# Attention pieces of later batches moved to other steps of two dense layers, and a few clears and loads issued later

## The chip, the cores and the metric

The kernel runs on one core of a Trainium2 chip, in one launch. The metric is the device time of one execution in microseconds (us). The kernel before has a median of 334.19 us over 3 runs (332.76 to 334.4). The engines' names in the profile are PE (TensorE, matmuls; PEld is its weight load), DVE (VectorE), ACT (ScalarE), POOL (GpSimd) and SP (SyncE). POOL and SP here mostly start DMAs. Each engine has one list of instructions, which it works off in the order in which the program issued them.

## The reference

```python
# q, k, v: (8 batches, 8 heads, 576 positions, 64), float32
scores = q @ k^T / 8                       # per batch and head
rel = i - j
heads 0..3:  keep 0 <= rel < 32
heads 4..7:  keep 0 <= rel < 128 and rel % 4 == 0
attn = softmax(scores where kept, else -1e9)
x = (attn @ v) as (4608 tokens, 512)
h = x @ w_in                               # 512 -> 2048
out = (h / (1 + exp(-h))) @ w_out          # 2048 -> 512, float32
```

## The kernel before

**Attention.** A batch `b` is worked in two halves `z`: `z = 0` are the plain heads 0 to 3, `z = 1` the dilated heads 4 to 7, whose positions are sorted into four classes by position modulo 4. For a half, these steps follow each other:

- `load_qk(b)` and `load_v(b)`: DMAs issued by POOL, 8 for q and k, 5 for v. `shift_v(b, ...)` copies parts of v to other partitions by DMA.
- `transpose(b, z, which, copies)`: PE turns q (`which = 0`) or k (`which = 1`) so that the head dimension lies on partitions (line 274, 36 or 24 small matmuls). The result, in two PSUM tiles, is copied to SBUF by `copies[0]` and `copies[1]` (line 278 for z = 0, line 287 for z = 1). `both` means one copy on DVE and the other on ACT.
- `scores(b, z)`: 72 or 80 small matmuls on PE (lines 324 and 336), then on DVE mask and scale (L448, L457) and a row maximum (L464).
- `exps(b, z, hi)`, once for `hi = 0` and once for `hi = 1`: 8 or 10 exponentials on ACT, each of 128x64 with its row sum (L496: one ACTIVATE and one ACTIVATION_READ_ACCUMULATOR). Where `shift` has subtracted the maximum on DVE beforehand (L474), it is one exponential of 128x640 (L487), and the sum is made on DVE (L505).
- `later(...)` holds the rest: `normal` (DVE: 1/sum and multiply, L509 to L512), `turn` (PE transposes, L521), `turned` (the copy of these, L529), `values` (PE, L554 and L618), `finish` (copies to `xT`, L631, L623, L625).

PSUM for all of this is a pool `ps` of 4 buffers. Where a tile takes a buffer again, the writer waits until every reader of the tile before is done; the same holds for the two buffers `n0`, `n1` of q and k.

**Dense layers.** For every batch, layer one makes 16 tiles `h` (L644, in batch 0 in two parts by `layer1_part`, L664), each followed by a SiLU on ACT into `gT` (L652, L671). Layer two multiplies `gT` with `w_out` into 128x512 tiles `o` (L705; in batch 0 L681), which DVE copies out (L690) and SP stores. PSUM for `h` and `o` is a pool `big` of 2 buffers.

**Order.** Batch 0's attention stands in a written-out list ahead of the loop. Everything else is spread by hand: `plan_of(b)` registers calls with `at(step, function, ...)`, and the loops over the dense layers of batch `b` call `plan(step)` ahead of each piece of their own work. Calls of one step are issued in the order in which they were registered. For batches 1 to 7 steps 0 to 15 stand ahead of the 16 tiles of layer one, and step 16 + n ahead of the n-th group of four matmuls of layer two. In batch 0 layer one runs from step -16 to 15, two steps to one call of `layer1_part` (two tiles of half a batch), and layer two again from 16. Steps that the loops don't reach are issued at the end of the batch. What a call issues goes to the end of each engine's list: a copy on ACT in step 17 stands behind every exponential of step 16.

The pieces that the change touches: `transposes(at, b, z, step)` issues both transposes of a half with `both` as copies, `all_exps(b, z)` puts the exponentials of a half at step 16, and `later(at, b, z, steps)` puts `normal` of `hi = 0` and `1` at the first two steps, `turn` and `turned` at the third, `values` and `finish` at the fourth. `clear_v(1, nc.vector)` is four memsets on DVE (L194 to L197) in the v buffer of batch 1.

Of the kernel before, what the change touches and what calls it, by code (L numbers as in the profile page):

```python
# [28 lines left out]
def kernel(  # L29
# [9 lines left out]
    nc = tc.nc  # L39
# [55 lines left out]
    def load_qk(b):  # L95

        for which in (0, 1):
            t = nat.tile([P, H * 8, D], F16, tag=f"n{which}", name=f"n{which}_{b}")
            u0, u1 = 2 * URS[0], 2 * (URS[0] + URS[1])
            qk[b, 0, which] = t[:, 0:u0].rearrange("p (h u) d -> p h u d", h=2)  # L100
            qk[b, 1, which] = t[:, u0:u1].rearrange("p (h u) d -> p h u d", h=2)
        for z in (1, 0) if b == 1 else (0, 1):
            for which, src in ((1, k), (0, q)):
                for i in (0, 1):
                    h = 2 * (2 * z + i)
                    nc.gpsimd.dma_start(  # L106
                        out=qk[b, z, which][i * HF : i * HF + UPS[z]].rearrange("p h u d -> p h (u d)"),
                        in_=src[b, h : h + 2].rearrange("h (p u) d -> p h (u d)", u=URS[z]),
                    )
# [13 lines left out]
    def load_v(b, pieces=("first", "second", "short", "plain")):  # L123
        vw = vws[b % 2]
        for m in (0, 1):
            if ("first", "second")[m] in pieces:
                nc.gpsimd.dma_start(  # L127
                    out=vw[KB:P, NP + m * ND : NP + (m + 1) * ND].rearrange("p (h r) d -> p h (r d)", r=DIL),
                    in_=v[b, HH:H, m * DIL * KB : (m + 1) * DIL * KB].rearrange("h (p r) d -> p h (r d)", r=DIL),
                )  # L130
        if "short" in pieces:
            lo = CL - W - TL
            for n in (0, 1):
                c = NP + 2 * ND + 2 * n * DIL
                nc.gpsimd.dma_start(
                    out=vw[n * KB : n * KB + W + TL, c : c + 2 * DIL].rearrange("p (h r) d -> p h (r d)", r=DIL),
                    in_=v[b, HH + 2 * n : HH + 2 * n + 2, lo * DIL : S].rearrange("h (p r) d -> p h (r d)", r=DIL),
                )
        if "plain" in pieces:
            nc.gpsimd.dma_start(  # L140
                out=vw[KB:P, 0:NP].rearrange("r (h m) d -> r h m d", h=HH),
                in_=v[b, 0:HH].rearrange("h (m r) d -> r h m d", r=KB),
            )
# [41 lines left out]
    def load_w_out(c):  # L185
        nc.gpsimd.dma_start(  # L186
            out=w_out16[:, 4 * c : 4 * c + 4, :],
            in_=moe_w_out[c * FC : (c + 1) * FC, :].rearrange("(c p) m -> p c m", p=P),
        )


    def clear_v(b, engine):
        vw = vws[b]
        engine.memset(vw[0:W, 0:NP].rearrange("p (h m) d -> p h m d", h=HH)[:, :, 0], 0.0)  # L194
        engine.memset(vw[0:W, NP : NP + ND], 0.0)
        for n in (0, 1):
            engine.memset(vw[n * KB + W : n * KB + KB, NP + 2 * ND :], 0.0)  # L197
# [210 lines left out]
    def scaled0(z, part):  # L408
        a = att(0)
        w = width(0, z, part)  # L410
        n = stat.tile([P, WM], F32, tag="nm", name=f"nms_0_{z}_{part}")
        nc.vector.tensor_scalar(n[:, 0:w], a["nm", z, part][:, 0:w], scale, None, ALU.mult)
        a["nm", z, part] = n
# [309 lines left out]
    def transposes(at, b, z, step):  # L723
        for which in (1, 0):
            at(step, transpose, b, z, which, both)

    def later(at, b, z, steps, copies=(nc.vector.tensor_copy, nc.vector.tensor_copy)):

        for hi in (0, 1):
            at(steps[hi], normal, b, z, hi)  # L730
        for hi in (0, 1):
            at(steps[2], turn, b, z, hi)
        for hi in (0, 1):
            at(steps[2], turned, b, z, hi, copies[hi])
        at(steps[3], values, b, z)
        at(steps[3], finish, b, z, copies)

    def plan_of(b):
        ev = {}

        def at(s, fn, *args):
            ev.setdefault(s, []).append((fn, args))

        def all_exps(b, z):
            for hi in (0, 1):
                at(16, exps, b, z, hi)

        if b == 0:

            at(-16, normal, 0, 1, 1)  # L750
            at(-15, shift_class, 0, dve, 1, 2)
            at(-14, normal, 0, 0, 1)
            at(-8, turn, 0, 1, 1)
            at(-8, turned, 0, 1, 1, act)
            at(-6, values0, 1, 1)
            at(-6, last_values, 0, 1, (1,))
            at(-6, finish0, 1, 1)
            at(-6, last_finish, 0, 1, 1)
            at(-4, turn, 0, 0, 1)
            at(-4, turned, 0, 0, 1)  # L760
            at(-2, values0, 0, 1)
            at(-2, last_values, 0, 0, (1,))
            at(-2, finish0, 0, 1, both)
            at(-2, last_finish, 0, 0, 1)
            transposes(at, 1, 1, 4)
            at(7, scores, 1, 1)
            for hi in (0, 1):
                at(7, shift, 1, 1, hi)
            transposes(at, 1, 0, 9)
            at(13, scores, 1, 0)  # L770
            at(14, shift_v, 1, nc.sync.dma_start)
            at(15, load_qk, 3)
            at(15, load_v, 2)
            at(15, shift_v, 2, nc.gpsimd.dma_start)
            all_exps(1, 1)
            all_exps(1, 0)
            later(at, 1, 1, (18, 19, 23, 25), both)
            later(at, 1, 0, (20, 23, 27, 29), both)
        elif b == 1:
            at(16, load_v, 3)  # L780
            at(16, shift_v, 3, nc.gpsimd.dma_start)
            transposes(at, 2, 0, 4)
            transposes(at, 2, 1, 10)
            transposes(at, 3, 0, 15)
            at(7, scores, 2, 0)
            at(17, load_qk, 4)
            at(13, scores, 2, 1)
            all_exps(2, 0)
            all_exps(2, 1)
            at(17, scores, 3, 0)  # L790
            at(18, exps, 3, 0, 0)
            at(18, exps, 3, 0, 1)
            later(at, 2, 0, (22, 24, 27, 28))
            later(at, 2, 1, (29, 31, 33, 34))
        else:
            if b + 2 < B:
                at(16, load_v, b + 2)
                at(16, shift_v, b + 2, nc.gpsimd.dma_start)
            if b + 1 < B:
                if b == 2:  # L800
                    for n in (0, 1):
                        at(1 + 2 * n, transpose, 3, 1, 1 - n, both)
                later(at, b + 1, 0, (0, 0, 4, 6))
                if b + 3 < B:
                    at(16, load_qk, b + 3)
            if b + 2 < B:
                transposes(at, b + 2, 0, 13)
                at(17, scores, b + 2, 0)
                at(18, exps, b + 2, 0, 0)
                at(18, exps, b + 2, 0, 1)  # L810
            if b + 1 < B:
                at(9, scores, b + 1, 1)
                all_exps(b + 1, 1)
                later(at, b + 1, 1, (22, 24, 27, 28))
            if b + 2 < B:
                transposes(at, b + 2, 1, 30)

        def plan(s):
            for fn, args in ev.pop(s, ()):
                fn(*args)  # L820

        return plan


    def keep_busy(tile, n):

        for _ in range(n):
            nc.tensor.matmul(
                tile[:, 0].rearrange("p (a c) -> p a c", c=P), ident,
                ident[:, None, :].broadcast_to([P, 4, P]), start=True, stop=True,  # L830
            )
# [13 lines left out]
    exps(0, 1, 0)  # L845
    maxima0(0, 0)
    scaled0(0, 0)
    clear_v(1, nc.vector)
    load_w_out(0)
    load_w_out(1)  # L850
    load_v(1)
    load_w_out(2)
    load_w_out(3)
    for which in (1, 0):
        transpose0(1, 1, which, act)
    normal(0, 1, 0)
# [24 lines left out]
    shift0(0, 1)  # L881
    exps(0, 0, 1)
    keep_busy(warm, 2)
    load_qk(2)

    for b in range(B):
        plan = plan_of(b)
        if b == 0:
            for x in range(NFF):
                plan(2 * x - NFF)  # L890
                plan(2 * x + 1 - NFF)
                layer1_part(2 * x % NFF, 2 * x // NFF, None if x else warm)
        else:
            for f in range(NFF):
                plan(f)
                layer1(b, f)
        if b == 0:
            layer2_first(plan)
        else:
            layer2(b, plan)  # L900
        for s in range(NFF, 3 * NFF):
            plan(s)
# [30 lines left out]
```

## Time and profile before

| what | before |
|---|---|
| median of 3 runs | 334.19 us (332.76 to 334.4) |
| profiled execution, its own time | 334.39 us |
| its span, first to last instruction | 332.6 us |
| PE busy | 313.6 us, 94% |
| ACT busy | 216.3 us, 65% |
| DVE busy | 179.0 us, 54% |
| POOL busy | 83.5 us, 25% |
| mean granted TensorE clock | 0.995 |

The profile is one execution. Times in its timeline count from the first instruction. "Chain" is the work that ended last, followed back from the end; "issue" is time in which an engine waited for nothing that the profile shows. A matmul group's busy time includes a modelled end. The profiled execution's own time is 1.8 us above its span.

### The profile page before, as it was taken

What the parts mean: (1) busy time and instruction counts of PE and PEld (TensorE: products, weight loads), DVE (VectorE), ACT (ScalarE), POOL (GpSimd) and SP (SyncE); (2) the same over time, 40 slices, a digit from 0 to 9 for tenths busy, and PEclk for the clock granted to TensorE, in tenths of its full rate; (3) what the DMA queues carried; (4) which work ended last, traced back from release to release, by engine and by line L of the source; (5) the groups of instructions that cost most, each with busy time, mean ns of one, the idle gap of its engine ahead of it and who ended that gap; (6) DMA issues with size and microseconds to landing.
All of it is one profiled execution on the core that took longest, in us unless ns stands there. A gap on an engine that the chain in (4) does not pass through costs nothing.

```text
span 332.6 us, 11772 instructions
## 1 busy us (share of the span) xinstructions
PE 313.6 (94%) x5151; PEld 202.5 (61%) x5151; DVE 179.0 (54%) x375; ACT 216.3 (65%) x703; POOL 83.5 (25%) x140
## 2 busy tenths in 40 slices
PE   5779889998999999999999979999999999999995
PEld 2548554576645776467745757468745676467643
DVE  5895756535668754673476443774557442530011
ACT  2765639465799858985799337995699357826300
POOL 8447527534200560056004700041000000000000
PEclk9999979999999999999999999999999999999999
DMA  8999999993811974197317960175001100110021
GB/s 110 187 212 203 191 229 205 136 217 61 129 66 65 128 124 67 66 160 121 68 42 112 180 111 2 65 97 109 4 34 65 63 4 0 66 65 0 2 95 64
DMA packets 45524, 32.63 MB, mean 98 GB/s; under 512 B 21248, under 2 KB 40192, under 8 KB 45472
## 3 DMA queue, kind: packets, MB, share of 16 engines
q0 software_dynamic: 39520, 21.73, 47.7%
q1 hardware_dynamic: 5952, 10.14, 8.4%
q8 instruction: 40, 0.66, 0.8%
q14 instruction: 12, 0.10, 0.1%
HBM read 37.75 MB, written 9.44 MB: 142 GB/s over the span
## 4 chain that ended last, share of the span: by engine, by line
PE 79%; DMA 8%; ACT 5%; issue 3%; POOL 2%; DVE 2%; POOLq 0%
PE h L644 34%; PE o L705 31%; DMA n<-in_k_dram 4%; ACT pe L496 4%; PE t L274 3%; PE x L554 3%; DMA vw<-in_v_dram 2%; DMA n<-in_q_dram 2%; PE pt L521 2%; PE o L681 2%; PE s L336 1%; PE s L324 1%; PE h L664 1%; POOL n L118 1%; POOL w_out L186 0%
## 5 line engine op out<-in xcount | busy, mean ns | idle before, releaser
L705 PE MATMUL o<-w_out,gT 128*128 128x512 f16 (+1 forms) x528 | 115.8, 373 | 0.5 <-DVE ob_last L714 0.5
L652 ACT ACTIVATE gT<-h 128x576 f16<-128x576 f32 x112 | 73.0, 651 | 66.2 <-PE h L644 65.5
L644 PE MATMUL h<-xT,w_in 128*128 128x288 f16 x896 | 115.4, 286 | 0.0
L644 PEld LDWEIGHTS <-w_in 128*128 128x128 f16 x896 | 85.7, 98 | 23.0 <-DVE ob L690 0.3
L705 PEld LDWEIGHTS <-gT 128*128 128x128 f16 x528 | 50.1, 98 | 53.6 <-issue 0.7
L496 ACT ACTIVATE pe<-ms,nm 128x64 f32<-128x64 f32 x246 | 81.6, 334 | 0.1
L690 DVE COPY ob<-o 128x512 f32<-128x512 f32 x35 | 24.1, 690 | 52.9 <-PE o L705 50.7
L496 ACT ACTIVATION_READ_ACCUMULATOR pe<-ms,nm 128x1 f32 x246 | 46.2, 188 | 0.0
L448 DVE SCALAR_TENSOR_TENSOR ms<-s,mask 128x512 f32<-128x512 f32 x28 | 19.2, 687 | 38.5 <-PE ss L324 18.9
L127 POOL DMA_DIRECT2D vw<-in_v_dram x16 | 10.1, 638 | 89.9 <-PE x L554 88.4
L512 DVE TENSOR_TENSOR pn<-pe,r 128x640 f16<-128x640 f32 (+2 forms) x32 | 25.3, 792 | 1.1
L631 DVE CAST xT<-x 128x512 f16<-128x512 f32 x26 | 16.8, 686 | 11.2 <-PE xs L618 11.2
L464 DVE TENSOR_REDUCE nm<-ms 128x10 f32<-128x640 f32 (+1 forms) x28 | 22.0, 787 | 1.0
L664 PE MATMUL h<-xT,w_in 128*128 128x256 f16 (+1 forms) x128 | 19.6, 307 | 2.9 <-issue 2.2
L106 POOL DMA_DIRECT2D n<-in_k_dram x28 | 16.5, 602 | 10.2 <-DMA w_in<-in_moe_w_in_dram 3.7
L106 POOL DMA_DIRECT2D n<-in_q_dram x28 | 16.5, 606 | 10.4 <-DMA w_out<-in_moe_w_out_dram 5.5
L671 ACT ACTIVATE gT<-h 128x512 f16<-128x512 f32 (+1 forms) x16 | 10.3, 650 | 11.7 <-PE h L664 11.6
L664 PEld LDWEIGHTS <-w_in 128*128 128x128 f16 x128 | 12.7, 104 | 7.8 <-issue 3.9
L529 DVE COPY ptT<-pt 128x640 f16<-128x640 f16 (+1 forms) x27 | 11.8, 470 | 10.2 <-PE pt L521 10.0
L681 PE MATMUL o<-w_out,gT 128*128 128x512 f16 x64 | 14.8, 379 | 0.0
L521 PE MATMUL pt<-ident,pn 128*128 128x128 f16 x152 | 12.2, 224 | 2.7 <-DVE pn L512 2.7
L274 PEld LDWEIGHTS <-n 64*64 64x64 f16 (+1 forms) x840 | 10.1, 101 | 5.6 <-issue 3.8
(102 smaller groups left out, 269.8 us busy)
## 6 DMA issues: line engine op xcount, KB each, us to landing
out_dram<-ob SPq DMA_DIRECT2D x35, 256.0 KB, 2.0
n<-in_k_dram POOLq DMA_DIRECT2D x28, 144.0 KB, 5.5
n<-in_q_dram POOLq DMA_DIRECT2D x28, 144.0 KB, 5.9
vw<-in_v_dram POOLq DMA_DIRECT2D x8, 288.0 KB, 6.7
vw<-in_v_dram POOLq DMA_DIRECT2D x16, 128.0 KB, 4.1
w_in<-in_moe_w_in_dram POOLq DMA_DIRECT2D x4, 512.0 KB, 11.7
w_out<-in_moe_w_out_dram POOLq DMA_DIRECT2D x4, 512.0 KB, 10.2
vw<-vw POOLq DMA_DIRECT2D x12, 128.0 KB, 3.1
```

The costliest lines, as they stand in the source:

```text
L106: nc.gpsimd.dma_start(out=qk[b, z, which][i * HF : i * HF + UPS[z]].rearrange("p h u d -> p h (u d)"), in_=src[b, h : h + 2].rearrange("h ...
L274: nc.tensor.transpose(dst, w, ident[r, r])
L448: nc.vector.scalar_tensor_tensor(out=ms[:, 0:8].rearrange("p (n t) c -> p n (t c)", n=2), in0=s[hi].rearrange("p n t c -> p n (t c)"), sca ...
L464: nc.vector.tensor_reduce(out=nm[:, 0:w], in_=ms[:, 0:w], axis=AX.X, op=ALU.max, negate=True)
L496: nc.scalar.activation(pe[:, t, :], slot(t), AF.Exp, scale=1.0 if b else scale, bias=nm[:, t : t + 1], accum_out=l[:, t : t + 1],)
L512: nc.vector.tensor_tensor(pn[:, 0:w], a["pe", z, hi][:, 0:w], r[:, 0:w, None].broadcast_to([P, w, KB]), ALU.mult)
L644: nc.tensor.matmul(h[:, half, 0:HS], w_in16[:, c, f * P : f * P + P], xT[:, c, half * HS : half * HS + HS], start=(c == 0), stop=(c == MC ...
L652: nc.scalar.activation(gT[:, f, s0 : s0 + S].rearrange("p (a c) -> p a c", a=2), h[:, :, 0:HS], AF.Silu)
L664: nc.tensor.matmul(h[:, i, 0 : c1 - c0], w_in16[:, c, (f + i) * P : (f + i + 1) * P], xT[:, c, c0:c1], start=(c == 0), stop=(c == MC - 1),)
L681: nc.tensor.matmul(o, gT[:, f, t * P : (t + 1) * P], w_out16[:, f, :], start=(f == 0), stop=(f == NFF - 1),)
L690: nc.vector.tensor_copy(ob, o)
L705: nc.tensor.matmul(o[:, part, 0:m] if last else o[:, 0], gT[:, f, t * P : (t + 1) * P], w_out16[:, f, part * m : (part + 1) * m] if last e ...
```

## The change

Nothing is added to or taken from the work; calls move.

- In batch 0: `transposes(1, 1)` from step 4 to 2, `scores(1, 1)` with its two `shift` from 7 to 8, `transposes(1, 0)` from 9 to 17, `scores(1, 0)` from 13 to 21, `exps(1, 0)` from 16 to 21, and the steps of both `later` by up to 3.
- In batch 1: `transposes(2, 0)` from 4 to 2, `transposes(2, 1)` from 10 to 9, `scores(2, 0)` from 7 to 6, `transposes(3, 0)` from 15 to 17, `scores(3, 0)` from 17 to 21, `exps(3, 0)` from 18 to 21.
- In batches 2 to 6: `scores(b + 1, 1)` from step 9 to 10.
- `clear_v(1)` goes from the list ahead of the loop to step -13 of batch 0, behind `normal(0, 0, 1)`, and the calls for the loads of `w_out`, of v of batch 1 and of q and k of batch 2 move with it. The order of the DMAs on POOL's queue stays the same.

```diff
             at(-14, normal, 0, 0, 1)
+            at(-13, clear_v, 1, nc.vector)
+            at(-13, load_v, 1)
+            for c in (2, 3):
+                at(-13, load_w_out, c)
+            at(-13, load_qk, 2)
...
-            transposes(at, 1, 1, 4)
-            at(7, scores, 1, 1)
+            transposes(at, 1, 1, 2)
+            at(8, scores, 1, 1)
             for hi in (0, 1):
-                at(7, shift, 1, 1, hi)
-            transposes(at, 1, 0, 9)
-            at(13, scores, 1, 0)
+                at(8, shift, 1, 1, hi)
+            transposes(at, 1, 0, 17)
+            at(21, scores, 1, 0)
...
             all_exps(1, 1)
-            all_exps(1, 0)
-            later(at, 1, 1, (18, 19, 23, 25), both)
-            later(at, 1, 0, (20, 23, 27, 29), both)
+            for hi in (0, 1):
+                at(21, exps, 1, 0, hi)
+            later(at, 1, 1, (18, 20, 24, 26), both)
+            later(at, 1, 0, (23, 25, 28, 30), both)
         elif b == 1:
...
-            transposes(at, 2, 0, 4)
-            transposes(at, 2, 1, 10)
-            transposes(at, 3, 0, 15)
-            at(7, scores, 2, 0)
+            transposes(at, 2, 0, 2)
+            transposes(at, 2, 1, 9)
+            transposes(at, 3, 0, 17)
+            at(6, scores, 2, 0)
             at(17, load_qk, 4)
             at(13, scores, 2, 1)
             all_exps(2, 0)
             all_exps(2, 1)
-            at(17, scores, 3, 0)
-            at(18, exps, 3, 0, 0)
-            at(18, exps, 3, 0, 1)
+            at(21, scores, 3, 0)
+            at(21, exps, 3, 0, 0)
+            at(21, exps, 3, 0, 1)
...
             if b + 1 < B:
-                at(9, scores, b + 1, 1)
+                at(10, scores, b + 1, 1)
...
     scaled0(0, 0)
-    clear_v(1, nc.vector)
-    load_w_out(0)
-    load_w_out(1)
-    load_v(1)
-    load_w_out(2)
-    load_w_out(3)
...
     keep_busy(warm, 2)
-    load_qk(2)
+    load_w_out(0)
+    load_w_out(1)
```

## The prediction

> **What bounds the kernel now.** I read the page first (busy time, clock, chain), then the chain in order of time with PE's waits, then ACT's timeline where layer two of batch 1 begins, then busy time by stage. The page says that PE is the bound:
>
> ```profile
> PE 313.6 (94%) x5151; PEld 202.5 (61%) x5151; DVE 179.0 (54%) x375; ACT 216.3 (65%) x703; POOL 83.5 (25%) x140
> PE 79%; DMA 8%; ACT 5%; issue 3%; POOL 2%; DVE 2%; POOLq 0%
> q8 instruction: 40, 0.66, 0.8%
> ```
>
> PE carries 79% of the chain, so a microsecond in which PE waits is a microsecond of the time unless a later wait swallows it. In the chain in order of time (start, length, what), PE pauses in batch 0 and hardly at all from there on:
>
> ```profile
> 39.79 0.47 PE t L274 x35
> 40.26 0.51 PE h L664 x3
> 40.77 2.25 issue
> 43.02 3.24 PE h L664 x13
> ...
> 88.00 1.09 PE h L644 x8
> 89.08 0.86 PE o L705 x4
> 89.95 0.61 PE s L324 x64
> 90.56 0.08 PE ss L324 x6
> 90.64 8.74 PE o L705 x40
> ```
>
> Layer one of batch 1 ends at 89.08; one group of layer two (0.86) and the scores of batch 3's plain heads (0.69) follow without a wait. What ACT does in that place, from its timeline:
>
> ```profile
> 87.27 0.63 ACT L278 COPY kT<-t 128x576 f16<-128x576 f16 x1
> 88.13 0.64 ACT L278 COPY qT<-t 128x576 f16<-128x576 f16 x1 [0.23 <-PE t L274]
> 89.12 0.65 ACT L652 ACTIVATE gT<-h 128x576 f16<-128x576 f32 x1 [0.35 <-PE h L644]
> 89.79 1.28 ACT L496 ACT_TABLE_LOAD   x1
> 91.08 0.35 ACT L496 ACTIVATE pe<-ms,nm 128x64 f32<-128x64 f32 x1
> ```
>
> The two copies of batch 3's k and q are made before the last SiLU; from 91.08 on ACT has exponentials alone, one every 0.33 us. The table by stage says how full ACT is there (columns: PE, PEld, DVE, ACT, POOL busy, clock, DMA share, GB/s):
>
> ```profile
> 43.49:46.90 3.41, 3.41 (x83) 1.95 (x81) 0.00 (x0) 1.31 (x2) 0.56 (x1) 0.50 1.22 244
> 89.08:109.89 20.81, 20.81 (x326) 10.71 (x324) 14.85 (x34) 20.72 (x115) 1.92 (x4) 1.00 0.19 60
> ```
>
> Layer two of batch 1: PE 20.81 of 20.81 us, ACT 20.72. Neither has slack. The first row shows the clock at half speed behind the pause of 2.25 us.
>
> **Batch 1: the copies behind the exponentials (+10.4).** `transposes(3, 0)` goes from step 15 to 17. Its copies on ACT now stand behind all of step 16, which is `exps` of batch 2: 8 + 10 + 10 + 10 = 38 exponentials. `scores(3, 0)`, now at step 21, reads for its second pair of heads the kT and qT that ACT copies, and PE works in order: behind that wait stand 15 groups of layer two and the turns and values of batch 2. Counted from the end of layer one (89.08 here):
> - ACT: 2.00 to the first exponential (91.08), 38 x 0.330 = 12.54 (spacing from 91.08 to 104.35, 40 exponentials later, is 0.332), copies about 1.2. Ready at 15.8.
> - PE: five groups of step 16 to 20, 5 x 0.86 = 4.30; transposes 0.76 (72 matmuls); first half of the scores 0.32. There at 5.4.
> - Wait: 15.8 - 5.4 = 10.4 us. DVE makes its own copies at once and can't shorten it.
>
> What is late next: the mask and maximum of these scores are 3.2 us on DVE (0.69 + 0.69 + 0.68 + 0.28 + 0.82) and stand ahead of `normal(2, 0, 1)` at step 24, whose turn is at 27. PE takes about 6 us to get there; I give it 0.9 of further wait, between 0 and 2. Nothing pays the 10.4 back, since from 109.89 on PE has no wait for ACT or DVE over 0.3 us until batch 7.
>
> **The clock behind a wait (+1.0 here).** After 2.25 us of pause, the half-speed stretch from 43.49 to 46.90 took 3.24 us for 13 matmuls that take 13 x 0.136 = 1.77 at full speed: 1.5 lost. A wait of 10.4 us will bring this on too; how much of it falls on work depends on when PE resumes. Bounds 0 and two such stretches (3.0); I take 1.0, as transposes and scores hardly slow (64 score matmuls took 0.72 instead of 0.61). [...]
>
> **Batch 0: pauses out, another in (-1.3).**
> - `clear_v(1)`: four memsets, 11.72 to 13.70 on DVE, leave the path to `normal(0, 1, 0)`. The first layer-one matmul (21.57) also waits for ACT, whose exponentials end at 15.5; of 2.0 us I take 0.9 (0 to 1.5). In their new place they lie in DVE's 1.56 us of idle before 28.63; at most 0.4 us sticks out, ahead of copies into xT. POOL's loads wait for them from about 30.4 on; they are done by then.
> - Loads: the order on POOL's queue is the same and the queue is DMA-bound up to 50 us, so `load_qk(2)` and `load_w_out` cost nothing. `load_qk(3)` must now wait for the later `transposes(1, 0)`; these run at about 44, its turn on the queue comes at 48.6. Cover gone: it and `load_v(2)` would slip by the excess, and batch 3's transposes need them only 40 us later.
> - Waits inside batch 0 (21.57 to 67.68) that go: 0.80 at `transposes(1, 0)` (until 39.59, when DVE's L457 is done with a PSUM buffer of the scores before), the pause 2.25, the clock 1.5, 0.65 and 0.62 in layer two: -5.8. Six tiles of layer one now run between `transposes(1, 1)` and their scores, eight between these and `transposes(1, 0)`.
> - New: `scores(1, 0)` at step 21. From the start of layer two: five groups and transposes 5.1, scores 0.7; DVE is busy with two `normal` of batch 1 until 7.6 (from 3.1 on, 2 x 2.25); mask and maximum 1.5 with their gaps; so exponentials start at 9.1, 18 x 0.33 = 6.0; then ACT's copy of the turned half (1, 1, 1), 0.67, which stands behind them: 15.8. PE reaches `values(1, 1)` at step 26 after ten groups 8.7 + 0.76 + 0.7 + 0.56 of turns = 10.8. Wait 5.0, and half clock behind it, +0.4 (the values are small).
> - Sum -0.9 - 5.8 + 5.0 + 0.4 = -1.3, bounds -4 and +2.
>
> **The pauses called issue (-1.5).** PE pauses at 40.77 (2.25), 75.90 (0.86) and 196.24 (1.88) with nothing to wait for. The trace's packets of the instruction queue q8 (40 of 16 KB; PE has 10,302 instructions) show why: one lands at 41.64, 75.43 and 196.69, and PE goes on 1.38, 1.33 and 1.43 later; the three places lie multiples of 256 instructions apart. So PE runs dry where it uses up 256 small instructions faster than the next block lands. The change puts more large matmuls among the small ones there (scores one tile later in every batch): I take 0.7 of the 0.86 and 0.8 of the 1.88 as gained, bounds 0 and 2.7. [...]
>
> **Sum.** 10.4 + 0.9 + 1.0 - 1.3 - 1.5 = +9.5. Made against the profiled execution: 334.39 + 9.5 = 343.9 us, 0.2 above what the median of 334.19 would give.
>
> **Rivals.**
> - *Slow clock after both waits.* If each of the two waits brings two full stretches of half speed over large matmuls, 2 x 3.0 - 1.4 = +4.6: 348.5. For it: 1.5 lost after only 2.25 of pause. Against: no other pause (1.88 at 196.24 included) shows a lower clock. Chance 0.12.
> - *Smaller wait.* Batch 0 gains its full 4 and both late pauses vanish (2.7), no slow clock: 10.4 + 0.9 - 4 - 2.7 = +4.6: 339.0. Chance 0.14.
> - *Faster: ACT's copies are not late.* The place is step 17 of batch 1, the price the 12.3 us of 10.4 + 0.9 + 1.0. If ACT reached the copies by the time PE has its first half of scores, the change would be -1.3 - 1.5 = -2.8: 331.6. That needs at most 5.4 - 2.00 - 1.2 = 2.2 us of exponentials ahead of them, 6 of 38. For it: in batch 0 the same move has only two short exponentials (L487, 1.36 us) ahead of the copies, and doesn't wait. Against: the order of the calls leaves 38 in front. Chance 0.04.
> - *No change to be seen.* The wait would have to be cut to about 3 us by the same way. Chance 0.02.
>
> **How the numbers follow.** Forecast 343.9 with 0.68. A measurement of this kernel can't tell less than about 0.5% (1.7 us) from no change. The range runs from the small wait to the slow clock, 339.0 to 348.5; it leaves out the fast cases and the ends of those two. Faster 0.04, same 0.02, slower 0.94.
>
> **What would show it.** In the profile after: a wait of some 10 us of PE at L324 for ACT's copy qT L278 near 95 us; ACT's exponentials without a gap before that copy; half clock behind it; a wait of about 5 us at L554 for ptT L529 near 52 us; no pause at 40 us. Wrong if PE passes `scores(3, 0)` without that wait, or if the stages from batch 2 on are shorter by more than 2 us.

## The result and the profile after

| | before | the change | ratio (95% interval) |
|---|---|---|---|
| first comparison, median of 4 runs each | 333.69 us (332.76 to 334.4) | 344.11 us (342.33 to 347.86) | 1.0296 (1.0242 to 1.0350) |
| second comparison | 334.79 us (11 runs) | 342.27 us (6 runs) | 1.0227 (1.0190 to 1.0263) |

The change is slower by 2.3 to 3.0%; 343.9 us were forecast, with a range of 339.0 to 348.5. The execution profiled in the first comparison was the slow one of its four (347.86 us, which the ratio leaves out), so what follows reads the profile of the second comparison: 343.62 us, span 341.8, clock 0.975. It is 1.35 us above the median beside it, so differences from the profile before come out larger here (+9.2) than the second ratio gives (+7.6). From its page, busy time and the chain by engine:

```profile
PE 315.3 (92%) x5151; PEld 203.3 (59%) x5151; DVE 178.8 (52%) x375; ACT 216.2 (63%) x703; POOL 83.4 (24%) x140
...
PE 79%; ACT 12%; DVE 4%; DMA 2%; issue 2%; POOL 1%; POOLq 0%; ACTq 0%
```

The work is the same. PE is busy for 315.3 us instead of 313.6, because more of it runs at half clock: in layer two of batch 1 alone, as the row below shows, PE is busy 23.89, where the same work at full speed takes 20.80 + 0.76. In the chain, ACT has gone from 5% to 12%. PE's waits name the place (us in total, times, longest):

```profile
PE s L324 <- ACT qT L278: 9.9, 1, 9.9
...
PE x L554 <- ACT ptT L529: 2.1, 1, 2.1
PE x L554 <- DVE ptT L529: 2.0, 1, 2.0
...
PE s L336 <- issue: 0.8, 1, 0.8
```

Left out are smaller waits, those of the first 19 us, and one of 1.1 for ACT's SiLU early in batch 0 (0.7 before). The wait for the copy `qT` is new, and so is the one for DVE's copy at L554, in batch 0; the one for ACT's at L554 was 0.6 before. The pause of 2.25 us at 40.77 is gone, and the one of 1.88 at 196.24 is 0.8. The chain in order of time (start, length, what) shows the long wait from the side that causes it:

```profile
86.78 1.28 ACT L496
88.06 0.01 issue
88.07 0.81 ACT pe L496 x5
88.89 0.10 issue
88.99 3.21 ACT pe L496 x20
92.20 0.10 issue
92.30 3.21 ACT pe L496 x20
95.52 0.10 issue
95.62 5.16 ACT pe L496 x31
100.77 0.52 ACT kT L278
101.29 0.54 ACT qT L278
101.83 0.04 issue
101.88 0.41 PE s L324 x30
102.30 0.17 PE ss L324 x7
102.46 7.18 PE o L705 x24
```

5 + 20 + 20 + 31 = 76 records are 38 exponentials of two instructions each. They run from 88.07 to 100.77 with holes of 0.10 us; the two copies stand behind them, and PE's second half of scores behind the copies. The 24 matmuls of layer two behind the wait take 7.18 us; at full speed, 0.86 for four as in the chain of before, they would take 5.2.

By stages, counted from the first dense matmul of each (so the times differ a little from those of the chain):

| stage | before | the change | difference | forecast |
|---|---|---|---|---|
| up to layer one of batch 1 | 67.52 | 66.31 | -1.21 | -1.3 |
| layer one of batch 1 | 21.40 | 19.60 | -1.80 | -0.7 - 0.76 (transposes that leave) = -1.46 |
| layer two of batch 1 | 20.80 | 34.08 | +13.28 | 10.4 + 0.9 + 1.0 + 0.76 (transposes that come) = +13.06 |
| batches 2 to 7 | 222.88 | 221.81 | -1.07 | -0.8 |
| span | 332.6 | 341.8 | +9.2 | +9.5 |

The stage table's row (us; then PE, PEld, DVE, ACT, POOL busy; clock; DMA share; GB/s) for layer two of batch 1 says the same: PE was full before (20.81 of 20.81), now it is busy 23.89 of 34.08, at a mean clock of 0.85.

```profile
85.91:119.99 34.08, 23.89 (x398) 11.81 (x395) 16.61 (x36) 23.04 (x117) 1.75 (x3) 0.85 0.13 40
```

### The profile page after: what moved, and what is told of

It is laid out like the page before. It is cut to its first block, busy times and chain, and to the rows that moved or that the text cites. A ratio compares the mean times of both kernels' runs of the same rounds, so it can differ in the third digit from the quotient of the medians.

```text
span 346.1 us, 11765 instructions
## 1 busy us (share of the span) xinstructions
PE 318.4 (92%) x5151; PEld 204.5 (59%) x5151; DVE 178.9 (52%) x375; ACT 216.4 (63%) x703; POOL 83.6 (24%) x140
## 4 chain that ended last, share of the span: by engine, by line
PE 80%; ACT 11%; DVE 3%; issue 2%; DMA 2%; POOL 1%; POOLq 0%; ACTq 0%
PE h L644 33%; PE o L705 29%; ACT pe L496 8%; PE h L664 4%; PE t L274 3%; PE x L554 3%; PE pt L521 2%; PE o L681 2%; DMA n<-in_q_dram 2%; PE s L336 1%; PE s L324 1%; ACT L496 1%; DVE pn L512 1%; PE x L580 1%; POOL n L118 1%
## 5 line engine op out<-in xcount | busy, mean ns | idle before, releaser
L705 PE MATMUL o<-w_out,gT 128*128 128x512 f16 (+1 forms) x528 | 118.2, 378 | 0.5 <-DVE ob_last L714 0.5
L644 PE MATMUL h<-xT,w_in 128*128 128x288 f16 x896 | 116.9, 289 | 0.0
L127 POOL DMA_DIRECT2D vw<-in_v_dram x16 | 10.1, 636 | 102.3 <-PE x L554 100.8
L664 PE MATMUL h<-xT,w_in 128*128 128x256 f16 (+1 forms) x128 | 18.0, 297 | 0.4 <-ACT gT L671 0.4
L529 DVE COPY ptT<-pt 128x640 f16<-128x640 f16 (+1 forms) x27 | 11.8, 469 | 12.2 <-PE pt L521 12.0
L324 PE MATMUL s<-kT,qT 64*32 64x64 f16 x520 | 5.9, 203 | 12.7 <-ACT qT L278 10.4
L681 PE MATMUL o<-w_out,gT 128*128 128x512 f16 x64 | 17.0, 414 | 0.0
L324 PEld LDWEIGHTS <-qT 64*32 64x32 f16 x576 | 5.0, 93 | 16.6 <-ACT qT L278 10.5
```

The lines of the kernel that those rows point to most:

```text
L644: nc.tensor.matmul(h[:, half, 0:HS], w_in16[:, c, f * P : f * P + P], xT[:, c, half * HS : half * HS + HS], start=(c == 0), stop=(c == MC ...
L664: nc.tensor.matmul(h[:, i, 0 : c1 - c0], w_in16[:, c, (f + i) * P : (f + i + 1) * P], xT[:, c, c0:c1], start=(c == 0), stop=(c == MC - 1),)
L681: nc.tensor.matmul(o, gT[:, f, t * P : (t + 1) * P], w_out16[:, f, :], start=(f == 0), stop=(f == NFF - 1),)
L705: nc.tensor.matmul(o[:, part, 0:m] if last else o[:, 0], gT[:, f, t * P : (t + 1) * P], w_out16[:, f, part * m : (part + 1) * m] if last e ...
```

## The experiments

**Theory:** the change's other moves gain about 3 us, and one call, `transposes(3, 0)` behind 38 exponentials on ACT, costs 12 to 13. **Rivals:** PE's later scores and DVE cost it, and not the copies; or the clock behind the waits is the larger part; or the other moved steps lose as well. The kernels were timed in three groups, each on a chip of its own and beside the kernel before: experiments 1 to 4 (its median there 335.26), 6 to 9 (334.63) and 5 (334.79). Ratios are to the kernel before of the same group, and differences in us are worked out from them. What is read from a profile rests on one execution of each kernel.

**1. Back to step 15.** The change, with the one call back in its old step.

```diff
-            transposes(at, 3, 0, 17)
+            transposes(at, 3, 0, 15)
```

> The changed kernel with one edit taken back: transposes(3, 0) of batch 1 stands at step 15 again, ahead of the exponentials of step 16; scores(3, 0) and exps(3, 0) stay at 21. Theory 'queue' (ACT's two copies stood behind 38 exponentials and PE waited for them): the wait of 10.4 us at L324 and the half-speed stretch behind it (2.3 us in the profile after) are gone, 331 to 333 us. Rival 'late scores' (scores and exponentials of batch 3 at 21 are what costs, since mask, exponentials and PSUM buffers come too late for layer two): 340 us or more, with PE waiting somewhere else in layer two of batch 1.

Measured: 332.18 us, ratio 0.9909 (0.9878 to 0.9940). Its chain at the same place has no ACT in it:

```profile
87.41 4.32 PE o L705 x20
91.73 0.61 PE s L324 x64
92.34 0.08 PE ss L324 x6
92.42 0.69 DVE ms L448
```

The scores follow the five groups of layer two at once. Layer two of batch 1 takes 21.41 us: 0.61 more than before the change, which is about what the later scores cost by themselves: 0.43 of it is a wait of PE at L521 for DVE's normalising, which now stands behind the mask and maximum of these scores. One call takes the kernel from 2 to 3% slower to 0.9% faster.

**2. Only this move.** The kernel before, with only the three calls for batch 3 moved.

```diff
-            transposes(at, 3, 0, 15)
+            transposes(at, 3, 0, 17)
...
-            at(17, scores, 3, 0)
-            at(18, exps, 3, 0, 0)
-            at(18, exps, 3, 0, 1)
+            at(21, scores, 3, 0)
+            at(21, exps, 3, 0, 0)
+            at(21, exps, 3, 0, 1)
```

> The kernel before with only this part of the change: transposes(3, 0) from step 15 to 17, scores(3, 0) from 17 to 21, exps(3, 0) from 18 to 21. Theory 'queue': the whole loss is here, 10.4 + 0.9 + 1.5 to 2.5 of clock on top of before: 345 to 348 us, above the changed kernel, since batch 0's part gave something back. Rival 'sum of many moves': less than half of the loss, below 340 us.

Measured: 348.69 us, ratio 1.0407 (1.0341 to 1.0472). Its waits and the end of its chain through ACT:

```profile
PE s L324 <- ACT qT L278: 10.4, 1, 10.4
```
```profile
102.94 0.52 ACT kT L278
103.46 0.54 ACT qT L278
104.04 0.41 PE s L324 x32
104.46 0.17 PE ss L324 x7
104.62 8.02 PE o L705 x24
```

The same wait, with nothing of the rest of the change: the move alone costs 13.6 us by the ratio (11.4 to 15.8). The 12.3 forecast lies in the interval; the time is 0.7 above the 345 to 348 expected, beside a kernel before that was 1.1 slower in this group. In its profile, layers one and two of batch 1 together are 12.2 us longer than before (54.35 for 42.20). Half clock elsewhere adds to it: 6.83 us of it instead of 3.41 behind the pause at 40.85, and 3.41 behind the pause of 1.84 at 209.51.

**3. At step 17, without ACT.** The change, with both copies of batch 3's plain heads on DVE.

```diff
-            transposes(at, 3, 0, 17)
+            for which in (1, 0):
+                at(17, transpose, 3, 0, which, (dve, dve))
```

> The changed kernel, with transposes(3, 0) left at step 17, but all four copies of its results on DVE instead of half of them on ACT. Theory 'queue': PE passes scores(3, 0) without a long wait, as in the run with step 15: 330 to 333 us; DVE has room (14.9 of 20.8 us busy in that stage before). Rival 'PSUM' (the transposes at 17 take all four PSUM buffers while others need them): still several us of wait at L274 or L324, 336 us or more.

Measured: 331.12 us, ratio 0.9892 (0.9838 to 0.9945). The step is as late as in the change and the scores too; only the engine of the copies differs, and the wait at L324 for `qT` is gone from the list. Its row of layer two of batch 1:

```profile
84.86:107.14 22.28, 21.84 (x398) 11.29 (x395) 17.86 (x38) 21.87 (x115) 1.76 (x3) 1.00 0.19 58
```

The stage is 1.48 longer than before: 0.76 for the transposes that now stand there, and 0.72, of which 0.43 is again the wait for DVE's normalising. So it is the queue on ACT, not the lateness of the step, and no PSUM buffer keeps PE waiting at L274 or L324 either.

**4. The place of the wait filled.** The change, with 44 matmuls of 128x512 ahead of step 21, into a half of `o` that nobody reads.

```diff
+                    if (b, x, f) == (1, 1, 4):
+                        for _ in range(44):
+                            nc.tensor.matmul(
+                                o[:, 1].rearrange("p (a c) -> p a c", c=P), ident,
+                                ident[:, None, :].broadcast_to([P, 4, P]), start=True, stop=True,
+                            )
```

> The changed kernel with 44 further matmuls of 128x512 ahead of step 21 in layer two of batch 1, into the unused half of the tile o (9.5 us at full speed), so that PE is busy for most of its wait. They take no part in the result. Theory 'clock behind a wait': the wait of 10.4 stays as time, but the half-speed stretch after it goes: 2 to 2.5 us under the changed kernel, 341 to 342 us, and the clock is at 1.00 from 95 to 125 us. Rival 'the clock falls for another reason' (the load of the exponentials, or chance): no faster than the changed kernel, 343.5 us or more.

Measured: 343.38 us, ratio 1.0252 (1.0189 to 1.0315). The half clock behind the wait is gone (no half speed between 62 and 340 us), and still the time isn't clearly below that of the change; it lies between the two expected figures. In the stage itself full speed shows:

```profile
85.41:118.11 32.70, 31.57 (x441) 15.62 (x439) 16.53 (x36) 23.04 (x117) 1.75 (x3) 1.00 0.15 43
```

It takes 32.70 us instead of 34.08, with PE going on after ACT's copy as late as in the change (16.0 us after the stage begins in both). In the chain behind it, two pauses are new, the first here:

```profile
134.18 0.52 PE t L274 x49
134.70 1.40 issue
136.10 0.38 PE t L274 x23
```

The second, 1.44 us, is at 171.84. Both break a run of 72 small transposes, in batches whose code the experiment didn't touch. The pause of 0.83 that the change has at 207.44 is gone in return. The 44 matmuls with their weight loads are 88 instructions, which shift all that follows against the blocks of 256 (the three pauses before lie whole multiples of 256 instructions apart); experiment 5 was made to tell whether that is the cause.

**5. Filled by a whole block.** As 4, but 128 matmuls of 128x192: 256 instructions.

```diff
-                        for _ in range(44):
+                        for _ in range(128):
                             nc.tensor.matmul(
-                                o[:, 1].rearrange("p (a c) -> p a c", c=P), ident,
-                                ident[:, None, :].broadcast_to([P, 4, P]), start=True, stop=True,
+                                o[:, 1, 0:192].rearrange("p (a c) -> p a c", c=64), ident,
+                                ident[:, None, 0:64].broadcast_to([P, 3, 64]), start=True, stop=True,
```

> The change, with the place of the long wait filled as in the fourth experiment, but by 128 matmuls of 128x192 instead of 44 of 128x512. Their results are read by nobody. With their weight loads they are 256 instructions on PE, one whole block, so that everything behind them lies at the same place in its block as in the change, where the 88 instructions of the fourth experiment moved it. Theory (the clock costs time behind the wait, and the fourth experiment gave that back in pauses at new block borders): no pause of 1.4 us near 134 and 172 us, no half clock between 95 and 125 us, and a time 2 to 5 us below the change run beside it, ratio to it 0.985 to 0.994. Rival (the pauses have nothing to do with the borders, or the half clock costs little): the same time as the fourth experiment, within 0.5% of the change. If the fill takes longer than the wait of 10.4 us, the excess comes on top.

Measured: 342.50 us, ratio 1.0215 (1.0173 to 1.0256), and beside it the change itself:

> The change itself, once more, for a profile of an execution that lies near its median. The prediction's theory: a wait of 10.4 us at L324 for the copy on ACT as before, one or two half-speed stretches behind it, and a stage of layer two of batch 1 of 32 to 34 us instead of 34.35. Rival, the profile of 347.86 was long for another cause (DMA, pauses): then this stage is 34.3 us again and the difference to the median lies in other stages. Ratio to the kernel before 1.024 to 1.035.

342.27 us, ratio 1.0227 (1.0190 to 1.0263); its profile is the one read above. From the chain of experiment 5, the run of transposes that paused in 4, and from the stage table its layer two of batch 1:

```profile
134.78 0.76 PE t L274 x72
```
```profile
85.88:118.71 32.83, 32.40 (x525) 21.89 (x523) 16.51 (x36) 23.04 (x117) 1.75 (x3) 1.00 0.13 40
```

The 72 transposes run through in 0.76, and at the second place too: the pauses follow the borders of the blocks. The traces show this more widely. Count PE's matmuls and weight loads in order in all twelve profiles: every pause of PE called issue that is 0.2 us or longer and comes after the first 19 us, 33 in all, falls on the same place in a block of 256, to within five instructions (remainders 185 to 189). Each ends 1.2 to 1.6 us after a packet of the instruction queue (q8) has landed; in experiment 4 these packets land at 134.77 and 171.78. Experiment 5, with 256 more instructions, has 41 such packets instead of 40.

The other half of the expectation missed: with a clock of 1.00 throughout, the stage is 32.83 instead of 34.08, and the whole no faster than the change. So the half clock was worth 1.25 us in this stage (1.38 by experiment 4), not 2 to 5. The fill here ends at 101.78, so PE reaches the second half of the scores some 0.3 us after ACT's copy is ready, which may be the difference between the two. Part of what full speed gives is taken back by DVE: PE now waits 0.43 us for DVE's normalising, as in experiments 1 and 3; in the change, half-speed matmuls had covered that wait. A pause at 206.16 is 1.59 in this profile and 0.83 in that of the change, which accounts for most of the rest.

The change itself came out a little under its expected ratio, and its stage of 34.08 just above the 32 to 34 expected. In the profile of the first comparison the stage is 34.42, so the rival of that expectation holds: the 4.3 us between the two profiles lie mostly in layer one of batch 1 (22.56 for 19.60), where that profile has a pause of 1.74.

**6. The clears alone.** The kernel before, with `clear_v(1)` and the loads at step -13 as in the change.

> The kernel before, with only the clears of batch 1's values behind the second part's normalising of batch 0, and the loads moved with them. The prediction's term: the clears leave DVE's way to the first layer-one matmul, 0.9 us off (bounds 0 and 1.5): 0.9 us below the kernel before, ratio 0.997; the trace after has that matmul at 20.14 instead of 21.57 us, so 20.1 here too. Rival, the gain is handed to the next wait: PE starts 1.4 us earlier, but waits the longer at 39.6 us for the PSUM buffer of the first scores of batch 1, or at the pause behind it, and the time stays within 0.2%: then layer one of batch 1 still starts near 67.7 us. If DVE's 2 us of clears in their new place delay what PE needs there, the time is above that of before by up to 0.5 us.

Measured: 333.49 us, ratio 0.9980 (0.9950 to 1.0011). The interval holds both the 0.9 us and nothing. The profile shows the start: first layer-one matmul at 19.93 instead of 21.57, layer one of batch 0 as long as before (27.61 and 27.58), layer one of batch 1 at 65.92 instead of 67.52. The waits in between are still there:

```profile
PE h L664 <- issue: 2.3, 1, 2.3
...
PE t L274 <- DVE ms L448: 0.8, 1, 0.8
```

They don't take the early start back in this profile.

**7. Batch 0 alone.** Experiment 6, with all steps of batch 0 as in the change.

> The kernel before, with the moved clears and with all steps moved in batch 0 as in the change, and nothing else (batch 1's and the later steps stay). The prediction's sum for batch 0: 1.3 us faster (bounds 4 faster, 2 slower), ratio 0.996, with a wait of 3 to 5 us at L554 for the turned half, and no wait at 39.6 us. Rival, the clock eats it: behind the wait at L554 stand two stretches of half clock of 1.7 us loss each, as the trace after has at 56 to 63 us, so that 0 to 2 us are lost and the ratio is 1.000 to 1.006. What the trace after shows of layer one of batch 1 (start at 67.30 instead of 67.68) speaks for about 0.4 us faster there even in that case; a longer pause without a cause at 74.7 us (1.74 instead of 0.86) would take it back.

Measured: 333.22 us, ratio 0.9930 (0.9899 to 0.9961), 2.3 us faster (1.3 to 3.4). From its chain:

```profile
49.40 6.09 ACT pe L496 x36
55.50 0.58 ACT ptT L529
56.08 0.04 issue
56.12 1.04 PE x L554 x48
```

The pause at 40 us and the wait ahead of it are gone, and in their place stand the 18 exponentials of step 21 (36 records), the copy behind them and PE behind the copy. Layer one of batch 0 falls from 27.58 to 20.91, layer two rises from 18.37 to 23.83, since transposes and scores have moved there too.

**8. The later scores alone.** The kernel before, with one step changed.

```diff
-                at(9, scores, b + 1, 1)
+                at(10, scores, b + 1, 1)
```

> The kernel before, with only the scores of the dilated heads one tile later (step 10 instead of 9) in the layers of batches 2 to 6. The prediction's term: the pause at 196.24 us, 1.88 long, falls by 0.8, and nothing else moves: 0.8 us faster, ratio 0.998. By the trace after, which has 0.86 there: 1.0 us faster. Rival: the pauses depend on where 256-instruction borders fall and on how long that one fetch takes on the day, not on the order of a tile; then the pause varies from profile to profile and the ratio is 1.000.

Measured: 333.32 us, ratio 0.9963 (0.9939 to 0.9986), 1.2 us faster (0.5 to 2.0). The pause in its chain:

```profile
195.86 0.59 PE s L336 x61
196.45 0.64 issue
197.09 0.21 PE s L336 x3
```

In the profile before, the same place reads:

```profile
195.58 0.61 PE s L336 x64
196.19 0.04 PE ss L336 x5
196.24 1.88 issue
198.12 0.27 PE ss L336 x11
```

0.64 instead of 1.88. One profile could be chance, so all are taken, save that of experiment 4, whose instructions are shifted by 88 and which has no pause there: at step 9 the waits list it with 1.9, 1.8, 1.7 and 1.7 us (before, experiments 2, 6, 7), at step 10 with 0.9, 0.8, 0.9, 1.4, 0.6, 1.6 and 1.3 (the change twice, experiments 1, 3, 8, 5, 9). The means are 1.8 and 1.1, and the two groups don't overlap. The fall of 0.7 lies within the 1.2 us (0.5 to 2.0) of the timed runs.

**9. A better version.** The change, with `transposes(3, 0)` at step 15 and batch 0's second new wait taken away: the turned dilated half of batch 1 and its copies to `xT` go to DVE, the plain half's steps come one or two later.

```diff
-            later(at, 1, 1, (18, 20, 24, 26), both)
-            later(at, 1, 0, (23, 25, 28, 30), both)
+            at(18, normal, 1, 1, 0)
+            at(20, normal, 1, 1, 1)
...
+                at(24, turned, 1, 1, hi, (dve, dve)[hi])
+            at(26, values, 1, 1)
+            at(26, finish, 1, 1, (dve, dve))
+            at(25, normal, 1, 0, 0)
+            at(26, normal, 1, 0, 1)
...
+                at(30, turned, 1, 0, hi, both[hi])
+            at(31, values, 1, 0)
+            at(31, finish, 1, 0, both)
...
-            transposes(at, 3, 0, 17)
+            transposes(at, 3, 0, 15)
```

> The change, with three edits: the transposes of batch 3's plain heads back at step 15 (as in the first experiment); in batch 0 the turned dilated half of batch 1 and its copies into xT on DVE alone, so that they don't stand behind the 18 exponentials of step 21 on ACT; and the turns of the plain half of batch 1 one to two steps later. The theory of waits and clock: the first experiment had 332.18; its trace has waits of 1.8 and 2.1 us at L554 in batch 0 and half clock behind them (1.7 us lost). With these gone 3 to 5.6 us come off: 326.6 to 329.2, ratio to the kernel before 0.975 to 0.985, no wait over 1 us at L554 before 67 us, and a clock above 0.99. Rival, DVE becomes late instead: DVE then makes four copies more while it has the normalising of both halves, PE waits for it at L554 or L521 just as long, and the time is that of the first experiment, 331 to 333.

Measured: 326.18 us, ratio 0.9750 (0.9724 to 0.9776), 8.4 us faster than the kernel before, the fastest of all and just under the 326.6 to 329.2 expected. Its longest waits after the first 19 us, and the row of batch 0's layer two:

```profile
PE s L336 <- issue: 1.3, 1, 1.3
PE pt L521 <- DVE pn L512: 0.8, 2, 0.4
PE s L336 <- ACT qC L308: 0.6, 1, 0.6
```
```profile
41.01:60.17 19.16, 18.80 (x381) 9.69 (x379) 16.31 (x34) 11.95 (x46) 10.66 (x18) 1.00 1.20 215
```

That layer takes 19.16 us; in experiment 1, with the copies on ACT and the plain half's steps earlier, it takes 24.21. Three copies more on DVE (378 instructions instead of 375; busy 16.31 of 19.16) don't make it late. The new engine and the later steps weren't tried apart. Layer one of batch 1 is 1.7 us shorter too, since pauses called issue of 0.73 and 1.02 in experiment 1 are 0.2 or less here.

## Why the prediction was right, step by step

- **The wait for `qT`, +10.4:** 9.9 in the profile above, 10.4 in that of the first comparison and in experiment 2. Both of its ends were placed well: ACT's copies end 15.9 us after layer two begins (15.8 forecast, 101.83 - 85.91), and PE stops for them 6.0 after (5.4 forecast). Experiments 1 and 3 show the cause twice, by the step and by the engine. Experiments 4 and 3 give the size: both have the later transposes and scores and a clock of 1.00, but only 4 has ACT's late copies, and their stages differ by 32.70 - 22.28 = 10.42.
- **DVE late behind it, +0.9, and the clock, +1.0:** experiment 3, without the long wait, still takes 0.72 more than the stage before and the moved transposes; so this lateness comes with the later scores and not only behind the wait. 0.43 of it is PE's wait at L521 that was forecast, the remainder has no row of its own. The clock is worth 34.08 - 32.70 = 1.38. The stage's 13.28 is then 0.76 + 0.72 + 10.42 + 1.38, step by step from one run to the next, and each step is near its forecast. The last two terms of the forecast aren't independent: the 24 matmuls behind the wait lose 2.0 at half speed, but slow matmuls cover DVE's lateness.
- **Batch 0, -1.3:** -1.21 in the profile, -2.3 (-3.4 to -1.3) in experiment 7. That the sum came out is partly luck, since its terms are off on both sides. The clears bring the first layer-one matmul forward by 1.25 in this profile and by 1.64 in experiment 6, not 0.9; the second figure is above the bound of 1.5. The new wait is 2.0 + 2.1 = 4.1, not 5.0, and its first part is for DVE's copy. Against it, the clock behind was taken at 0.4: 6.83 us ran at half speed, 8 matmuls at L681 took 3.53 us where 8 take 1.83 at full speed, and the turns behind them 0.84 instead of 0.50: 2.0 lost. With the -5.8 of old waits as forecast, -1.25 - 5.8 + 4.1 + 2.0 = -0.95; what makes the rest of the -1.21 has no row of its own. Experiments 1 and 3, with batch 0 as in the change but one slow window less, start layer one of batch 1 2.5 and 2.3 us earlier than before.
- **The pauses, -1.5:** -0.8 for the later scores is borne out by experiment 8: 0.7 between the profiles, 1.2 (0.5 to 2.0) between the timed runs. The -0.7 in layer one of batch 1 isn't. That stage takes 21.40 in the profile before, but 20.43, 20.13 and 20.13 in experiments 6, 7 and 8, which change nothing in it; without the transposes that leave (0.76), that is 19.4 to 19.7, and the change has 19.60. So the stage's -1.80, close to the -1.46 forecast, is the transposes and a profile before that happened to be long there: luck. The pause itself (0.86 at 75.90 before) is 0.44 in the change, 1.74 in the profile of the first comparison and missing in experiments 6 to 8.
- **Batches 2 to 7** are 1.07 shorter, under the 2 us that would have spoken against the prediction.
- **The rivals.** The slow clock did come after both waits, but it cost 2.0 us behind the one and 1.25 to 1.38 behind the other, not 3.0 each, so 348.5 wasn't reached. The faster rival was priced at -2.8 if ACT weren't late; experiments 1 and 3 made that case: 3.0 and 3.6 us faster.
- **The gain that the wait buried:** batch 0 -2.3, the scores -1.2, the move of batch 3's calls +13.6 add up to +10.1 from runs of each part; the remaining moves of batch 1 have no run of their own. The change itself gave 9.9 (8.1 to 11.7) in the first comparison and 7.6 (6.4 to 8.8) in the second.

The clears alone couldn't be told from no change by the timed runs. Why the pause at 75.90 comes in some executions and not in others is only partly answered: the packet of its block took 3.01 us in the profile before and 0.88 to 1.24 in experiments 6 to 8, but 0.93 in the profile of the first comparison, which has the pause of 1.74. What makes a packet start or land late is open.

## What to carry to other kernels

A copy that moves a few steps later costs what has meanwhile been queued ahead of it on its engine (38 exponentials here, and 9.9 us of wait): count the instructions between its old and its new place on each queue, and compare the end of that queue with the moment when the engine that waits needs the result (here 15.9 and 6.0 us into the stage, and 24 matmuls of layer two stood behind the wait). Where a step must be late, give its copies to the engine whose queue is short there. When several moves are bundled, undo them one at a time; here one call hid a gain of 0.9% and pointed the way to 2.5%.

## What the runs showed of the hardware

**In these profiles the clock fell and rose on a grid of 3.41 us.** The half-speed stretches lasted 3.41 (before), 6.83 and 10.24 (the change) and 13.65 us (experiment 2): one, two, three or four times 3.41. Within a profile their starts lie whole multiples of 3.41 apart too (55.06 and 96.02 in the change: 12 times; 56.23, 76.71 and 100.60 in the profile of the first comparison: 6 and 13 times from the first). The stretch around the long wait began at 96.02, 4.1 us into the wait, and ended at 106.26, 4.4 after PE had resumed at 101.88. By these profiles, how many windows stay slow depends on how much of the window in which PE resumes is work. Cutting the stretches into equal windows, the one from 55.49 in experiment 7 held work for its last 2.78 us (PE resumed at 56.12), and full speed came at its end; in experiment 2 the one from 103.30 held 2.67 (resumed at 104.04), and the change's one from 55.06 held 1.94 (resumed at 56.53), and after both a further window was slow. So the same wait costs one slow window or two, by its phase: layer two of batch 0 took 23.83, 24.21 and 24.24 us with one (experiments 7, 1, 3), and 25.09, 25.26 and 25.23 with two (the change, experiments 4, 5). A pause of 2.25 us, with PE busy for 1.24 of the 3.49 us up to 43.49, was enough for the stretch that began there in the profile before.

**The place of an instruction in PE's list mattered.** Adding 88 instructions to PE's list in batch 1 made two pauses of 1.4 us in batches 2 and 3; adding 256 at the same point made none there. All 33 pauses of this kind in the twelve profiles stand at the same place in a block of 256 (remainders 185 to 189), and PE goes on 1.2 to 1.6 us after a packet of the instruction queue lands.
